# Two weight matrices of a gated MLP: w_out loaded in runs of seven rows, w_in read with a step of seven

## The chip, the cores and the metric

The kernel runs on one core of a Trainium2 chip. The metric is the device time of one execution in microseconds; the time of a kernel is the median over its runs. Before the change it is 667.86 us (three runs, 667.57 to 667.94). A core has a matrix engine (TensorE; in the profile PE for its matmuls, PEld for its weight loads), VectorE (DVE), ScalarE (ACT), GpSimd (POOL), SyncE (SP), which issues nearly all transfers here, and 16 DMA engines that carry them out. On-chip memory has 128 partitions.

## The reference

One decode step, for 4 sequences with one token each and 512 features, of a block with two halves. The first is attention of 32 heads over a cache of 4096 positions; the second, which the change touches, is a small gated MLP. All inputs are bf16.

```python
def _B_ref(x, w_in, w_sp, b_sp, w_out):
    z = _gelu(jnp.einsum('bsd,df->bsf', x, w_in))        # w_in: 512 x 1792
    z1 = z[..., :Fh].copy()                              # Fh = 896
    z2 = _layernorm(z[..., Fh:], axis=-1)
    g = jnp.einsum('ts,bsf->btf', w_sp, z2) + b_sp[None, :, None]
    return jnp.einsum('bsf,fd->bsd', z1 * g, w_out)      # w_out: 896 x 512

mod = (_silu(c) @ w_mod).reshape(c.shape[0], 6, 1, -1)   # sa, ca, ga, sb, cb, gb
h = _layernorm(x, axis=-1) * (1 + ca) + sa
x = x + ga * _A_ref(h, A_k_cache, A_v_cache, A_wq, A_wo)
h = _layernorm(x, axis=-1) * (1 + cb) + sb
x = x + gb * _B_ref(h, B_w_in, B_w_sp, B_b_sp, B_w_out)
```

The sums over the 896 hidden features (the layer norm's mean and square, and the product with w_out) do not depend on the order in which the features are stored, as long as z1, z2 and the rows of w_out share it.

## The kernel before

**The stream.** The caches are 268 MB of the 283 MB that are read. The loop `for i in range(NT)` (line 530) goes over 32 steps, each for four heads of one sequence. In a step VectorE multiplies a 4 MB tile of keys by the query (`mult`, line 288), TensorE sums it with an identity matrix as weights (`reduce_d`, line 294), VectorE and ScalarE form the softmax (`sum8`, `scores`), and two steps later TensorE multiplies by the values (`pv`, line 366). The order of the instructions on every engine is that of the program text, written out by hand (`manual_schedule`). The tiles `kt` and `vt` have two buffers each. All large transfers are issued by SP in one order, and the DMA engines take them in that order.

**The weights of the second half.** In step 30 (`if i == L - 1`, line 594) SP issues, behind the last value tile, which goes in five pieces, the transfers of `win_sb` (w_in, 1792 KB, line 597), `wout_sb` (w_out, 896 KB, line 599) and `wg_sb` (the last sixth of w_mod, 512 KB, line 602, into a buffer of `vt`, so that the profile calls it `vt`). In `win_sb` partition p holds rows 4p to 4p + 3 of w_in, each with all 1792 columns. In `wout_sb` partition p holds, in place j of NH = 7, row 128 j + p of w_out: seven rows of 1 KB that lie 128 rows apart in DRAM.

**The end.** After the loop the last pieces of values are worked off as they come (`o_last`, line 393), the attention's output is projected (line 418) and added to x, and `normed` and what follows give `hT2`, the second half's input with features on partitions (DJ = 4 groups of 128, times B = 4). Then:

- `gate(1)` and `gate(0)` (line 679) multiply by w_in: for each of seven groups f of 128 hidden features, and each k of four, one matmul (line 684) with 128 columns of `win_sb` as weights and `hT2[:, k, :]`, four columns wide, streamed. Group f holds columns `n0` to `n0 + 127`, `n0 = (h * NH + f) * P`. So hidden feature 128 f + p is on partition p, in place f.
- ScalarE takes the GELU of both halves (lines 691 and 695), after which it loads another table (line 696). Line 697 sums z2 and its square over partitions with a matmul.
- VectorE forms `zz` (line 700), the product of z1 with ones and with z2, and line 707 multiplies it by w_out: 4 groups of output features times seven places f, with `wout_sb[:, f, ...]` as weights, 128 contiguous columns each.
- Line 715 multiplies the conditioning by `wg_sb`. Lines 719 to 731 and ScalarE's lines 201 and 202 give the layer norm's scale `rs3`; lines 735 to 748 put the parts together, line 748 with the result of line 715; line 750 transposes, line 752 adds x, and SP stores the output (line 753).

Other weights are read with a step too: line 242 takes columns of `wm_sb` with a step of DJ = 4, as lines 418 and 483 do of w_o, and line 499 reads `accR`, fp32, with the same step of 4 elements.

Of the kernel before, what the change touches and what calls it, by code (L numbers as in the profile page):

```python
# [24 lines left out]
def kernel(  # L25
# [16 lines left out]
    nc = tc.nc  # L42
    P = 128
# [3 lines left out]
    FH = F // 2  # L47
    DJ = D // P
    NF = F // P
    NH = FH // P  # L50
# [22 lines left out]
    def ps_sm(shape, dtype=F32):  # L73
        return psum.tile(shape, dtype, name="sm", bufs=3)
# [37 lines left out]
    def load_v(i):  # L112
# [30 lines left out]
        out=sel32, in_=ident_f.rearrange("p (q r) -> p r q", r=R), axis=AX.X, op=ALU.add  # L143
# [10 lines left out]
    for g in range(G):  # L154
        nc.vector.tensor_reduce(out=selg[:, g:g + 1], in_=idr[:, g], axis=AX.XY, op=ALU.add)
    nc.vector.tensor_reduce(
        out=sel4, in_=ident_f.rearrange("p (c b) -> p b c", b=B), axis=AX.X, op=ALU.add
# [3 lines left out]
        out=mask8, in_=ident_f.rearrange("p (h u) -> p h u", h=2 * HQ), axis=AX.X, op=ALU.add  # L161
# [42 lines left out]
    def normed(pool, src, name, then=None, last=None):  # L204
# [24 lines left out]
        out=sg, in0=cx, scalar1=-60.0, scalar2=-1.0, op0=ALU.max, op1=ALU.mult  # L229
# [6 lines left out]
    def mod_cols(s0, n, dst):  # L236
# [20 lines left out]
        out=hs, in0=modA[:, DJ:2 * DJ, :], scalar=1.0, in1=xn, op0=ALU.add, op1=ALU.mult  # L257
# [27 lines left out]
    def mult(i, kc):  # L285
        kt = kts[i][:, kc * KC:(kc + 1) * KC, :]
        g, b = divmod(i, B)
        nc.vector.tensor_tensor(out=kt, in0=kt, in1=bc(qbc[:, g, b, :], KC), op=ALU.mult)  # L288
# [19 lines left out]
    def scores(i):  # L308
        sum8(i, 1)
        S = st.pop((i, "S"))  # L310
        mrow = wk.tile([P, 1], F32, name="mrow")
        nc.vector.tensor_reduce(out=mrow, in_=S, axis=AX.X, op=ALU.max)  # L312
        mb = wk.tile([P, R], F32, name="mb")
        nc.vector.tensor_copy(out=mb, in_=mrow.to_broadcast([P, R]))  # L314
        mt = wk.tile([P, R], F32, name="mt")
        nc.vector.transpose(mt, mb)  # L316
        nM = wk.tile([P, 1], F32, name="nM")
        nc.vector.tensor_reduce(out=nM, in_=mt, axis=AX.X, op=ALU.max)  # L318
        nc.vector.tensor_scalar(  # L319
            out=nM, in0=nM, scalar1=-att_scale, scalar2=None, op0=ALU.mult  # L320
        )
        pbd = pbds[i % 3]
        rs = wk.tile([P, 1], F32, name="rs", bufs=3)
        for q in range(HQ):
            r = slice(R * q, R * (q + 1))
            nc.scalar.activation(  # L326
                out=pbd[r, :, q], in_=S[r, :], func=AF.Exp, bias=nM[r, :],
                scale=att_scale, accum_out=rs[r, :],
            )
        st[i, "rs"] = rs  # L330
# [23 lines left out]
    def norm_b(i):  # L354
        if whole(i):
            z = st.pop((i, "z"))
            rz = wk.tile([P, z.shape[1], HQ], F32, name=f"rz{z.shape[1]}", bufs=2)
            nc.vector.reciprocal(out=rz, in_=z)
            st[i, "rz"] = rz
# [24 lines left out]
    def o_cols(i):  # L384
        op = ps_sm([P, HQ])
        nc.tensor.matmul(op, lhsT=st.pop((i, "osb")), rhs=sel4, start=True, stop=True)  # L386
        st[i, "op"] = op
# [44 lines left out]
    for n in set(SETS):  # L432
        picks[n] = consts.tile([P, n, P], BF16, name=f"pick{n}")
        for a in range(n):
            u = P // n
            nc.vector.tensor_copy(
                out=picks[n][:, :, a * u:(a + 1) * u],
                in_=ident_bf.rearrange("p (u r) -> p r u", r=n),
# [65 lines left out]
    def rows_up():  # L504
        if "rows" in st:
            wp, k = st.pop("rows")
            if k == 0:
                nc.vector.tensor_copy(out=accR, in_=wp)
            else:
                nc.vector.tensor_tensor(out=accR, in0=accR, in1=wp, op=ALU.add)  # L510
            if SETS[k + 1] == HQ:
                st["turn"] = True
# [12 lines left out]
    def add_up():  # L525
        while adds:
            o_add(*adds.pop(0))

    QPLAN = {0: (1, 2), 1: (3, 4, 5), 2: (6, 7)}
    for i in range(NT):  # L530
        more = list(QPLAN.get(i, ()))
        mult(i, 0)
        if i >= 1:
            scores(i - 1)
        if i >= 2:
            norm_b(i - 2)
        add_up()
        rows_up()
        dealt()
        if i >= 3:  # L540
            o_pick(i - 3)
        reduce_d(i, 0)
        if i >= 3:
            o_cols(i - 3)
        if more:
            queries(more.pop(0))
        mult(i, 1)
        if i >= 1:
            norm_r(i - 1)
        if i >= 3:  # L550
            o_scale(i - 3)
        sum8(i, 0)
        reduce_d(i, 1)
        load_k(i + 2)
        if i >= 1:
            norm_a(i - 1)
        project()
        if i - 3 in ends:
            deal(ends[i - 3])
        while more:  # L560
            queries(more.pop(0))
        if i >= 2:
            pv(i - 2)
        if i == 0:
            load_v(1)
        elif 2 <= i < L:
            load_v(i)
        if i == 2:
            nc.scalar.dma_start(out=sp_t[:, 0:1], in_=B_w_sp[0:1, 0:1])
            nc.scalar.dma_start(out=sp_t[:, 1:2], in_=B_b_sp.rearrange("(a b) -> a b", b=1))  # L570
            mps = ps_sm([P, 3 * DJ, B])
            mod_cols(2, 3 * DJ, mps)
            nc.vector.tensor_copy(out=modT, in_=mps)
            pre_cm.__exit__(None, None, None)
            wts = tl = ctx.enter_context(tc.tile_pool(name="wts", bufs=1))
            wo_sb = wts.tile([P, H - HQ, D], BF16, name="wo_sb")
            wo_last = wts.tile([P, HQ, D], BF16, name="wo_last")
            hl = (H - HQ) * DH
            h0 = 0
            for n in SETS:  # L580
                nc.sync.dma_start(
                    out=wo_sb[:, h0:h0 + n, :],
                    in_=A_wo[h0 * DH:(h0 + n) * DH].rearrange("(p r) n -> p r n", p=P),
                )
                h0 += n
            nc.sync.dma_start(out=wo_last, in_=A_wo[hl:H * DH].rearrange("(q p) n -> p q n", p=P))
        if i == 5:
            sps = ps_sm([P, 2])
            nc.tensor.matmul(sps, lhsT=ones_b, rhs=sp_t, start=True, stop=True)
            nc.vector.tensor_copy(out=spf, in_=sps)  # L590
            nc.vector.tensor_copy(out=g8[:, 1, :], in_=spf[:, 0:1].to_broadcast([P, B]))
            cbT = modT[:, 2 * DJ:3 * DJ, :]
            nc.vector.tensor_scalar_add(out=cbT, in0=cbT, scalar1=1.0)
        if i == L - 1:
            load_v(L)
            win_sb = wts.tile([P, DJ, F], BF16, name="win_sb")
            nc.sync.dma_start(out=win_sb, in_=B_w_in.rearrange("(p j) n -> p j n", p=P))
            wout_sb = wts.tile([P, NH, D], BF16, name="wout_sb")
            nc.sync.dma_start(out=wout_sb, in_=B_w_out.rearrange("(j p) n -> p j n", p=P))
            wg_sb = kvp.tile([P, NJ, DH], BF16, name="vt", bufs=2)  # L600
            wg_sb = wg_sb.rearrange("p n d -> p (n d)")[:, 0:DJ * D].rearrange("p (k n) -> p k n", k=DJ)
            nc.sync.dma_start(out=wg_sb, in_=wm[:, :, 5 * D:])
# [26 lines left out]
    def sums():  # L629
# [13 lines left out]
    hT2 = tl.tile([P, DJ, B], BF16, name="hT2")  # L643
# [7 lines left out]
        out=nv2, in0=mq2[:, 0:1], scalar=mq2[:, 0:1], in1=mq2[:, 1:2],  # L651
# [7 lines left out]
        out=hl, in0=xs, scalar=mq2[:, 0:1], in1=cbT[:, :, BL], op0=ALU.subtract, op1=ALU.mult  # L659
    )  # L660
    nc.vector.scalar_tensor_tensor(
        out=hT2[:, :, BL], in0=hl, scalar=rsl, in1=sbT[:, :, BL], op0=ALU.mult, op1=ALU.add
# [4 lines left out]
        out=x1m, in0=x1[:, :, :, None].to_broadcast([P, DJ, B, HQ]),  # L667
# [11 lines left out]
    def gate(h):  # L679
        z = ps_red()[:, 0:NH * B].rearrange("p (f b) -> p f b", b=B)  # L680
        for f in range(NH):
            for k in range(DJ):
                n0 = (h * NH + f) * P
                nc.tensor.matmul(
                    z[:, f, :], lhsT=win_sb[:, k, n0:n0 + P], rhs=hT2[:, k, :],
                    start=(k == 0), stop=(k == DJ - 1),
                )
        return z.rearrange("p f b -> p b f")
# [12 lines left out]
        out=zz.rearrange("p f g b -> p g b f"), in0=z1[:, None].to_broadcast([P, 2, B, NH]),  # L701
# [11 lines left out]
    for j in range(DJ):  # L713
# [7 lines left out]
        out=mq3, in_=ps3.rearrange("p (g b f) -> p g b f", g=2, b=B), axis=AX.X, op=ALU.add  # L721
# [4 lines left out]
        out=rs3, in0=mq3[:, 1], scalar=LN_EPS, in1=rs3, op0=ALU.add, op1=ALU.subtract  # L726
# [3 lines left out]
        out=g8[:, 0, :], in0=mq3[:, 0, :], scalar=-1.0, in1=g8[:, 1, :], op0=ALU.mult, op1=ALU.mult  # L730
# [5 lines left out]
        out=t3[:, 2], in0=yb[:, 0], scalar1=spf[:, 1:2], scalar2=None, op0=ALU.mult  # L736
    )
    nc.vector.tensor_tensor(
        out=g8, in0=g8, in1=rs3[:, None, :].to_broadcast([P, 2, B]), op=ALU.mult
    )  # L740
    nc.vector.tensor_tensor(
        out=t3[:, 0:2], in0=g8[:, :, :, None].to_broadcast([P, 2, B, DJ]), in1=yb, op=ALU.mult
# [3 lines left out]
        out=tt, in_=t3.rearrange("p g b j -> p b j g"), axis=AX.X, op=ALU.add  # L746
# [37 lines left out]
```

## Time and profile before

| | |
|---|---|
| median of 3 runs | 667.86 us |
| span of the profiled execution, first to last instruction | 665.8 us |
| read from memory in that span | 282.73 MB, 425 GB/s |
| busy: TensorE / its weight loads | 399.3 us (60%) / 175.4 us (26%) |
| busy: VectorE / ScalarE / GpSimd | 419.5 us (63%) / 85.0 us (13%) / 3.8 us (1%) |
| w_out: issue to landing | 26.5 us |

The times of all views are microseconds from the first instruction. A span runs from the first to the last instruction; the device time is some 2 us longer than it. The page divides the span into 40 slices and gives for each the busy tenths of every engine, the granted TensorE clock in tenths of full speed, and the share of DMA. The stretches at the end, with what each engine did (busy us, and instructions begun, in brackets):

```profile
core 0: us, PE busy (x) PEld busy (x) DVE busy (x) ACT busy (x) POOL busy (x), PEclk, DMA share, GB/s
646.70:653.20 6.50, 5.07 (x138) 4.74 (x135) 2.79 (x12) 0.00 (x0) 0.00 (x0) 0.50 1.02 425
653.20:657.70 4.50, 2.68 (x44) 2.34 (x44) 1.78 (x10) 1.74 (x5) 1.08 (x5) 0.50 0.94 354
657.70:660.00 2.30, 2.17 (x58) 2.00 (x58) 0.49 (x3) 1.16 (x4) 0.00 (x0) 0.50 0.56 199
660.00:661.40 1.40, 0.91 (x29) 0.92 (x30) 0.83 (x6) 1.36 (x3) 0.00 (x0) 0.50 0.24 78
661.40:663.20 1.80, 0.95 (x17) 0.57 (x17) 1.01 (x5) 0.02 (x1) 0.00 (x0) 0.50 0.00 0
```

The DMA engines run to about 661 us; the last 16 do not end together, so their share falls over several microseconds.

### The profile page before, as it was taken

What the parts mean: (1) busy time and instruction counts of PE and PEld (TensorE: products, weight loads), DVE (VectorE), ACT (ScalarE), POOL (GpSimd) and SP (SyncE); (2) the same over time, 40 slices, a digit from 0 to 9 for tenths busy, and PEclk for the clock granted to TensorE, in tenths of its full rate; (3) what the DMA queues carried; (4) which work ended last, traced back from release to release, by engine and by line L of the source; (5) the groups of instructions that cost most, each with busy time, mean ns of one, the idle gap of its engine ahead of it and who ended that gap; (6) DMA issues with size and microseconds to landing.
All of it is one profiled execution on the core that took longest, in us unless ns stands there. A gap on an engine that the chain in (4) does not pass through costs nothing.

```text
span 665.8 us, 6509 instructions
## 1 busy us (share of the span) xinstructions
PE 399.3 (60%) x2674; PEld 175.4 (26%) x2674; DVE 419.5 (63%) x589; ACT 85.0 (13%) x278; POOL 3.8 (1%) x17
## 2 busy tenths in 40 slices
PE   1195795556556746754665467566555468666675
PEld 0132331222222312222222222222222223322245
DVE  3485592776565777655567756657765566776833
ACT  1021120111011111101111110111111011111112
POOL 1000000000000000000000000000000000000000
PEclk9998987777898778789877778787777897887975
DMA  8999999999999999999999999999999999999996
GB/s 363 452 419 433 431 417 435 436 437 422 439 432 438 422 439 433 436 423 436 435 431 426 438 435 432 426 436 437 431 426 437 435 429 432 433 436 421 438 419 234
DMA packets 13377, 283.15 MB, mean 425 GB/s; under 512 B 1308, under 2 KB 3236, under 8 KB 4132
## 3 DMA queue, kind: packets, MB, share of 16 engines
q1 hardware_dynamic: 13328, 282.73, 98.9%
q8 instruction: 21, 0.34, 0.2%
q14 instruction: 8, 0.07, 0.0%
q10 hardware_dynamic: 20, 0.01, 0.0%
HBM read 282.73 MB, written 0.00 MB: 425 GB/s over the span
## 4 chain that ended last, share of the span: by engine, by line
DMA 56%; DVE 28%; PE 13%; issue 1%; SPq 1%; ACT 0%; DVEq 0%
DMA kt<-in_A_k_cache_dram 52%; DVE kt L288 21%; PE red L294 11%; DMA win_sb<-in_B_w_in_dram 5%; DVE osb L378 2%; DVE S L303 1%; DVE mrow L312 1%; DVE osb L374 1%; PE ops L366 1%; SPq L104 1%; DVE mt L316 1%; DVE nM L318 0%; PE qps L274 0%; DVE mb L314 0%; DVE nM L319 0%
## 5 line engine op out<-in xcount | busy, mean ns | idle before, releaser
L294 PE MATMUL red<-kt,ident_bf 128*128 128x512 bf16 x1024 | 301.5, 461 | 236.4 <-DVE kt L288 236.4
L288 DVE TENSOR_TENSOR kt<-kt,qbc 128x8192 bf16<-128x8192 bf16 x64 | 282.8, 4420 | 185.2 <-DMA kt<-in_A_k_cache_dram 184.2
L294 PEld LDWEIGHTS <-ident_bf 128*128 128x128 bf16 x1024 | 118.9, 116 | 411.5 <-issue 285.8
L326 ACT ACTIVATE pbd<-S,nM 32x128 bf16<-32x128 f32 x128 | 73.8, 577 | 505.3 <-DVE nM L319 463.2
L366 PE MATMUL ops<-vt,pbd 128*16 128x512 bf16 x992 | 62.6, 388 | 1.4 <-DMA vt<-in_A_v_cache_dram 1.4
L303 DVE TENSOR_REDUCE S<-red 128x64 f32<-128x512 f32 x64 | 43.8, 684 | 5.8 <-PE red L294 5.8
L378 DVE SCALAR_TENSOR_TENSOR osb<-ops,selg,osb 128x128 f32<-128x128 f32 x93 | 32.6, 351 | 3.3
L326 ACT ACTIVATION_READ_ACCUMULATOR pbd<-S,nM 32x1 f32 x128 | 32.0, 250 | 0.0
L366 PEld LDWEIGHTS <-pbd 128*16 128x16 bf16 x992 | 23.2, 90 | 30.7 <-issue 8.5
L386 PEld LDWEIGHTS sm<-sel,osb 128*128 128x128 f32 x62 | 11.7, 194 | 7.4 <-issue 2.2
L374 DVE TENSOR_SCALAR osb<-ops,selg 128x128 f32<-128x128 f32 x31 | 10.1, 325 | 5.3 <-PE ops L366 5.3
L386 PE MATMUL sm<-sel,osb 128*128 128x4 f32 x62 | 9.2, 219 | 2.1 <-DVE osb L378 2.0
L278 ACT CAST qbc<-qps 128x512 bf16<-128x512 f32 x8 | 4.7, 585 | 45.3 <-PE qps L274 45.3
L274 PE MATMUL qps<-wq_sb,hTb 128*32 128x512 bf16 x128 | 9.2, 412 | 1.6 <-DVE hTb L262 0.9
L312 DVE TENSOR_REDUCE mrow<-S 128x1 f32<-128x128 f32 x32 | 9.2, 286 | 1.1
L242 PE MATMUL sm<-cT,wm_sb 128*128 128x4 bf16 x80 | 3.0, 173 | 8.3 <-DMA wm_sb<-in_w_mod_dram 8.3
L316 DVE STREAM_TRANSPOSE mt<-mb 128x32 f32<-128x32 f32 x32 | 6.8, 212 | 1.1
L337 DVE TENSOR_SCALAR rsb<-mask,rs 128x4 f32<-128x4 f32 x32 | 7.2, 224 | 0.4 <-ACT pbd L326 0.4
L318 DVE TENSOR_REDUCE nM<-mt 128x1 f32<-128x32 f32 x32 | 6.0, 186 | 1.1
L314 DVE COPY mb<-mrow 128x32 f32<-128x32 f32 x32 | 5.8, 181 | 1.1
L491 PE MATMUL sm<-wo_sb,od 128*4 128x512 bf16 x24 | 5.7, 379 | 0.0
L319 DVE TENSOR_SCALAR nM<-nM 128x1 f32<-128x1 f32 x32 | 4.9, 153 | 1.1
(136 smaller groups left out, 88.8 us busy)
## 6 DMA issues: line engine op xcount, KB each, us to landing
kt<-in_A_k_cache_dram SPq DMA_DIRECT2D x31, 4096.0 KB, 23.0
vt<-in_A_v_cache_dram SPq DMA_DIRECT2D x31, 4096.0 KB, 30.7
wq_sb<-in_A_wq_dram SPq DMA_DIRECT2D x1, 4096.0 KB, 12.3
kt<-in_A_k_cache_dram SPq DMA_DIRECT2D x2, 2048.0 KB, 16.7
wo_sb<-in_A_wo_dram SPq DMA_DIRECT2D x3, 1024.0 KB, 22.9
kt<-in_A_v_cache_dram SPq DMA_DIRECT2D x3, 1024.0 KB, 25.5
wm_sb<-in_w_mod_dram SPq DMA_DIRECT2D x1, 2560.0 KB
win_sb<-in_B_w_in_dram SPq DMA_DIRECT2D x1, 1792.0 KB
```

The costliest lines, as they stand in the source:

```text
L274: nc.tensor.matmul(qp[R * q:R * (q + 1)], lhsT=hTb[:, k, b, :], rhs=wq_v[:, k, gs, q, :], start=(k == 0), stop=(k == DJ - 1), tile_positio ...
L288: nc.vector.tensor_tensor(out=kt, in0=kt, in1=bc(qbc[:, g, b, :], KC), op=ALU.mult)
L294: nc.tensor.matmul(red, lhsT=ident_bf, rhs=kt[:, :, m * RD:(m + 1) * RD], start=(m == 0), stop=(m == DH // RD - 1),)
L303: nc.vector.tensor_reduce(out=st[i, "S"][:, kc * KC:(kc + 1) * KC], in_=st.pop((i, "red", kc)), axis=AX.X, op=ALU.add,)
L312: nc.vector.tensor_reduce(out=mrow, in_=S, axis=AX.X, op=ALU.max)
L316: nc.vector.transpose(mt, mb)
L326: nc.scalar.activation(out=pbd[r, :, q], in_=S[r, :], func=AF.Exp, bias=nM[r, :], scale=att_scale, accum_out=rs[r, :],)
L337: nc.vector.tensor_scalar(out=st[g, "rsb"][:, b, :], in0=mask4, scalar1=st.pop((i, "rs")), scalar2=None, op0=ALU.mult)
L366: nc.tensor.matmul(opss[i % 2][g:g + G * HQ], lhsT=pbds[i % 3][:, n, :], rhs=vts[i][:, n, :], start=(m < 4), stop=(m >= NJ // G - 4), tile ...
L374: nc.vector.tensor_scalar(out=osb, in0=ops[:, 0, :], scalar1=selg[:, 0:1], scalar2=None, op0=ALU.mult)
L378: nc.vector.scalar_tensor_tensor(out=osb, in0=ops[:, g, :], scalar=selg[:, g:g + 1], in1=osb, op0=ALU.mult, op1=ALU.add,)
L386: nc.tensor.matmul(op, lhsT=st.pop((i, "osb")), rhs=sel4, start=True, stop=True)
```

## The change

`wout_sb` gets another arrangement: partition p holds rows 7p to 7p + 6 of w_out, which are neighbours in DRAM, in places f = 0 to 6. So that the hidden features agree, group f of `gate` no longer takes 128 neighbouring columns of w_in but every seventh one from column f of its half: hidden feature 7p + f is on partition p, in place f. The transfer of w_in, the number of instructions and the shapes of all tiles stay. Lines 691 to 707 are untouched; they work place by place.

```diff
             wout_sb = wts.tile([P, NH, D], BF16, name="wout_sb")
-            nc.sync.dma_start(out=wout_sb, in_=B_w_out.rearrange("(j p) n -> p j n", p=P))
+            nc.sync.dma_start(out=wout_sb, in_=B_w_out.rearrange("(p f) n -> p f n", p=P))
...
         for f in range(NH):
             for k in range(DJ):
-                n0 = (h * NH + f) * P
+                n0 = h * FH + f
                 nc.tensor.matmul(
-                    z[:, f, :], lhsT=win_sb[:, k, n0:n0 + P], rhs=hT2[:, k, :],
+                    z[:, f, :], lhsT=win_sb[:, k, n0:n0 + (P - 1) * NH + 1:NH], rhs=hT2[:, k, :],
                     start=(k == 0), stop=(k == DJ - 1),
                 )
```

## The prediction

> **What bounds the kernel now.** I read the page first: its span, the rows of the 40 slices, and the shares of the chain of waits.
>
> ```profile
> span 665.8 us, 6509 instructions
> PEclk9998987777898778789877778787777897887975
> DMA  8999999999999999999999999999999999999996
> DMA 56%; DVE 28%; PE 13%; issue 1%; SPq 1%; ACT 0%; DVEq 0%
> ```
>
> The DMA engines are busy in every slice but the last: the kernel streams the caches, and its end is whatever follows the last transfers. The granted clock has fallen to a half at the end. So the change must be judged in the last 9 us, and the second view is the chain of waits there, in order of time (start, length, what).
>
> ```profile
> 625.92 31.81 DMA win_sb<-in_B_w_in_dram
> 657.73 0.05 issue
> 657.78 1.67 PE red L684 x56
> 659.45 0.02 issue
> 659.47 0.19 ACT z L695
> 659.66 0.02 issue
> 659.68 1.28 ACT L696
> 660.96 0.01 issue
> 660.97 0.21 ACT rs L201
> ```
>
> The arrival of w_in lets the gate go at 657.73, its 56 matmuls of line 684 stand wholly on the chain, and then come ScalarE's GELU, a table load of 1.28 us, the reciprocal root, and some VectorE steps. w_out and the last slice of w_mod, the transfers behind w_in, are not on it. The third view is the timeline, for how close they come (in brackets idle time before, and what ended it).
>
> ```profile
> 659.69 0.40 DVE L700 TENSOR_TENSOR zz<-z,st 128x56 bf16<-128x56 f32 x1 [0.56 <-ACT z L695]
> 660.06 0.89 PEld L707 LDWEIGHTS <-wout_sb 128*128 128x128 bf16 x28 [0.29 <-DMA wout_sb<-in_B_w_out_dram]
> 660.15 0.89 PE L707 MATMUL qps<-zz,wout_sb 128*128 128x8 bf16 x28 [0.20 <-DVE zz L700]
> 661.38 0.58 PE L715 MATMUL sm<-cT,vt 128*128 128x4 bf16 x16 [0.34 <-DMA vt<-in_w_mod_dram]
> 661.87 0.21 DVE L745 TENSOR_REDUCE tt<-t 128x16 f32<-128x48 f32 x1
> 662.18 0.17 DVE L748 TENSOR_TENSOR tt<-tt,sm 128x16 f32<-128x16 f32 x1
> ```
>
> w_out is there at 660.06, and its matmuls start at 660.15, after zz (659.69 + 0.40 = 660.09): a near tie, which zz ends. The w_mod slice comes last, at 661.38; its matmuls are over at 661.96, while VectorE reaches their reader (line 748) only after line 745 ends at 662.08. So both late transfers have a little slack, 0.1 us or less, and the table load is what the end waits for.
>
> **The change, part by part.**
>
> **The load of w_out.** One DMA instruction on SP before and after, of 0.38 us at 633.5; nothing is moved past another queue. In DRAM a partition's share was seven runs of 1 KB and becomes one of 7 KB. The trace's records of single packets price this: 896 packets of 1 KB take 46 ns each, so 56 on each of 16 engines are 2.6 us; w_in's 14 KB packets take 535 ns and the 8 KB ones of the value cache 309, so a straight line between 4 KB (159 ns) and 8 KB gives about 272 ns for 7 KB, and eight of them are 2.2 us: 0.4 us less per engine. The late engines decide: the last packet of w_in ends at 657.31 and w_out's 56 follow until about 659.68, which is 2.37 us, so the last engine gains 2.37 - 2.18 = 0.2 us, for w_out and for the slice behind it. Engines that are earlier gain more, and nobody waits for them. Worth: nothing, because zz releases line 707 and the table load covers line 715. If the gate cost nothing and that cover were gone, the 0.1 us between 662.08 and 662.18 is all that the arrival could return. I take 0, with bounds -0.2 and 0. w_in lies ahead of w_out in SP's queue, and its packets are unchanged, so 657.73 stays; only early engines, which now draw larger packets while late ones still fetch w_in, could push it. The packets of 14 KB took 535 ns early and late (two of about 1.0 us apart), so I take 0, with +0.3 as the upper bound, which is how far the last engine stands behind the one before it (657.31 against 656.99).
>
> SP's issue of the w_mod slice took 6.26 us at 643.2, behind a full queue; with 768 packets fewer ahead it may be shorter. Its packets move only after 655, so this is worth 0.
>
> **The reads of w_out (line 707).** The same 28 matmuls on contiguous columns: 0. That z, z1 and zz now hold the features in another order changes no shape: lines 691 to 702 and the sums over features cost the same.
>
> **The columns of w_in (line 684).** All 56 weight loads read 128 columns at a step of seven elements (14 bytes) instead of one. No row of the trace has that step. The neighbours are steps of one and of four, and one fp32 load with columns 16 bytes apart:
>
> ```profile
> 657.78 1.65 PE L684 MATMUL red<-hT,win_sb 128*128 128x4 bf16 x56 [0.78 <-DMA win_sb<-in_B_w_in_dram]
> 76.63 1.76 PE L242 MATMUL sm<-cT,wm_sb 128*128 128x4 bf16 x48
> 649.79 0.67 PE L418 MATMUL sm<-oTs,wo_last 128*128 128x3 bf16 x16 [0.25 <-DVE oTs L408]
> 581.64 1.94 PEld L499 LDWEIGHTS sm<-ident_f,qbc 4*128 4x128 f32 x8
> 653.57 0.50 PEld L192 LDWEIGHTS sm<-sq_ln,inv_d 128*128 128x128 f32 x2
> ```
>
> The pitch of a load-and-matmul pair is the group's length less its last member's, over the members less one. Step one: (1.65 - 0.166) / 55 = 27 ns. Step four: line 242, (1.76 - 0.173) / 47 = 33.8 ns at full clock, and line 418, (0.67 - 0.172) / 15 = 33 ns at half clock. The step thus costs some 6.5 ns a pair, with the matmul as narrow as the gate's and whatever the clock. For step seven I see three readings, by the bytes of a partition that one load spans: 256 at step one, 1024 at step four, 1792 at step seven.
>
> First, a surcharge on what is spanned beyond 256 bytes: 6.5 ns for 768 more, so 13 ns for 1536 more, 40 ns a pair, 56 x 13 = +0.7 us. Second, a rate: step one has a floor of its own, and step four is already bound by its span, 33.3 ns for 1024 bytes, which makes 33.3 x 1.75 = 58 ns, 56 x 31.3 = +1.75 us. Third, the fp32 rows: line 499 has (1.94 - 0.322) / 7 = 231 ns a load, against about 0.50 - 0.31 = 0.19 us for a contiguous one; that is 41 ns for 2048 - 512 = 1536 bytes more, just the excess of our step, so 68 ns a pair and +2.3 us. That row has another type, four partitions, and only a pair to compare with, but it speaks against the smallest reading. I take the middle, 58 ns. The lower end is 27 ns (nothing; no row has a step that is quicker than none), the upper end the contiguous fp32 load at 0.19 us, 56 x 163 = +9.1 us, far off since bf16 at step four is nowhere near it.
>
> [...]
>
> All 56 pairs are on the chain: gate(1) delays line 691, gate(0) follows on TensorE and delays line 695, and behind it, on ScalarE, the table load, and then lines 201 and 202; on TensorE the sum of line 697 and then line 707, 715 and 750. Nothing beside them can take the delay up, since w_in's arrival starts the pairs and the table load waits for the last. No wait is added.
>
> **Sum.** 0 for the load, +1.75 us for the gate. The profiled execution has a span of 665.8 us, so 667.5 is due there; the median of the runs, 667.86, is 2.1 us more, which lies around the span and stays. Forecast: 667.86 + 1.75 = 669.6 us.
>
> **The rivals.** **(B) The step is cheap**, the surcharge reading or less, a pitch of 33 (as step four) to 50 ns: +0.35 to +1.3 us, 668.2 to 669.2, in the middle 668.6. For it: the two bf16 rows as they stand. Against it: the fp32 row.
>
> **(C) The step is dear**, 68 ns or more: +2.3 us, 670.2; with loads that lose their fast path altogether, toward the fp32 end (677). For it: line 499; the step is odd, so every second column starts at an odd multiple of two bytes, while all step-four columns are aligned to eight. Against the far end: line 418's loads are 118 ns long against 104, no other kind of load. [...]
>
> **(D) Not slower: the load of weights keeps its pitch at any step, and w_out's shorter transfer is what is left.** Then line 715 starts 0.1 to 0.2 us sooner, and it decides only if line 748 in truth waits for it: 667.7 to 667.9. For it: 661.38 is a DMA's release. Against it: 33 ns at step four, and 662.08 comes after 661.96. [...]
>
> That the load isn't done in 7 KB runs I hold unlikely: w_in's 14 KB runs go as one packet each.
>
> **How the numbers follow.** Forecast (50 to 63 ns) 0.42; B 0.30; C 0.18, of it 0.06 beyond 671; D 0.10. A measurement of this kernel tells 0.2%, 1.34 us, from no change; the line is at 50.6 ns. Faster by more needs an arrival that the trace doesn't show: 0.03. Within: B and the rest of D, 0.37. Slower: the forecast and C, 0.60. The range leaves out D and the far part of C: 668.0 to 671.0.
>
> **What would show it.** Line 684's 56 matmuls take 58 x 55 + 170 = 3.4 us instead of 1.65, from a start that is still at about 657.7; the table load of line 696 then starts at about 661.4. Packets of 7 KB replace w_out's, and neither line 707 nor line 715 waits for a DMA. I am wrong if line 684 stays below 2.9 us (B), goes beyond 3.8 (C), or if w_in's arrival moves.

## The result, and the profile after

The median of 12 runs is 669.34 us (668.86 to 669.97), against 667.60 us (667.28 to 668.40) in 12 runs of the kernel before: a ratio of 1.0025, 95% interval 1.0017 to 1.0034, or +1.7 us (1.1 to 2.3). The page of the kernel after has the same picture of the whole, with 768 packets fewer (12609 against 13377):

```profile
span 667.2 us, 6509 instructions
PEclk9998988777798778778977779888777897777975
DMA  8999999999999999999999999999999999999994
DMA packets 12609, 283.15 MB, mean 424 GB/s; under 512 B 1308, under 2 KB 2340, under 8 KB 3364
DMA 60%; DVE 28%; PE 10%; issue 1%; SPq 0%; ACT 0%; DVEq 0%
```

The same chain of waits at the end, in order of time (start, length, what):

```profile
625.33 32.31 DMA win_sb<-in_B_w_in_dram
657.64 0.04 issue
657.68 3.16 PE red L684 x56
660.85 0.02 issue
660.87 0.19 ACT z L695
661.06 0.02 issue
661.08 1.28 ACT L696
662.36 0.01 issue
662.38 0.21 ACT rs L201
```

The chain has the same links. w_in arrives at 657.64, 0.1 us earlier than before; line 684 takes 3.16 us where it took 1.67, and every link behind it has its old length. The timeline around it:

```profile
657.68 3.15 PE L684 MATMUL red<-hT,win_sb 128*128 128x4 bf16 x56 [0.39 <-DMA win_sb<-in_B_w_in_dram]
661.55 0.89 PE L707 MATMUL qps<-zz,wout_sb 128*128 128x8 bf16 x28 [0.20 <-DVE zz L700]
662.30 0.57 PE L715 MATMUL sm<-cT,vt 128*128 128x4 bf16 x16
663.59 0.17 DVE L748 TENSOR_TENSOR tt<-tt,sm 128x16 f32<-128x16 f32 x1
```

A pair now takes (3.15 - 0.193) / 55 = 53.8 ns; from its second pair on, the pitch is 53.3. Line 707 waits for zz alone and line 715 for nothing: both transfers behind w_in are in before they are wanted. The last VectorE step, line 752, moved from 662.83 to 664.23, 1.40 us: the 1.49 us of line 684 less the 0.1 us by which w_in came sooner in this execution.

### The profile page after: what moved, and what is told of

It reads as the page before. It is cut to its first block, busy times and chain, and to the rows that moved or that the text cites. A ratio compares the mean times of both kernels' runs of the same rounds, so it can differ in the third digit from the quotient of the medians.

```text
span 667.2 us, 6509 instructions
## 1 busy us (share of the span) xinstructions
PE 396.6 (59%) x2674; PEld 175.2 (26%) x2674; DVE 419.3 (63%) x589; ACT 85.0 (13%) x278; POOL 3.8 (1%) x17
## 2 busy tenths in 40 slices
DMA packets 12609, 283.15 MB, mean 424 GB/s; under 512 B 1308, under 2 KB 2340, under 8 KB 3364
## 4 chain that ended last, share of the span: by engine, by line
DMA 60%; DVE 28%; PE 10%; issue 1%; SPq 0%; ACT 0%; DVEq 0%
DMA kt<-in_A_k_cache_dram 55%; DVE kt L288 21%; PE red L294 9%; DMA win_sb<-in_B_w_in_dram 5%; DVE osb L378 2%; DVE S L303 1%; DVE mrow L312 1%; DVE mt L316 1%; DVE osb L374 0%; PE red L684 0%; DVE nM L318 0%; DVE mb L314 0%; DVE nM L319 0%; SPq L104 0%; ACT L696 0%
## 5 line engine op out<-in xcount | busy, mean ns | idle before, releaser
L294 PE MATMUL red<-kt,ident_bf 128*128 128x512 bf16 x1024 | 296.4, 455 | 239.7 <-DVE kt L288 239.7
L294 PEld LDWEIGHTS <-ident_bf 128*128 128x128 bf16 x1024 | 117.3, 115 | 411.6 <-issue 278.7
```

Source lines behind the costliest of these rows:

```text
L294: nc.tensor.matmul(red, lhsT=ident_bf, rhs=kt[:, :, m * RD:(m + 1) * RD], start=(m == 0), stop=(m == DH // RD - 1),)
```

## The experiments

The theory to test: the 56 weight loads are the whole loss, and the new transfer is worth nothing because it is hidden. The rivals: that the transfer has a share of its own (the median moved 1.7 us, the gate 1.5); that gate(1) has room; and three laws for what a step costs.

**One part alone: the load.** The edit against the kernel before:

```diff
-  nc.sync.dma_start(out=wout_sb, in_=B_w_out.rearrange("(j p) n -> p j n", p=P))
+  nc.sync.dma_start(out=wout_sb, in_=B_w_out.rearrange("(p f) n -> p f n", p=P))
```

> The new load of w_out without the step in the reads of w_in (so z1 and z2 meet other rows of w_out than in the reference; the work is the same). Theory, the weight loads are everything: no change, ratio within 0.05% of 1, line 684 at 1.65 us. Rival, the larger packets also move the end: faster by 0.1 to 0.2 us (0.02 to 0.03%) if line 748 waits for line 715; slower by 0.25 us (0.04%) if the early engines' larger packets delay the arrival of w_in, which would fill the gap between the 1.49 us that line 684 grew in the trace and the 1.74 us that the median moved.

667.89 us in 11 runs beside 667.55 in 27 of before: ratio 1.0002 (0.9994 to 1.0011), no difference that the interval of -0.4 to +0.7 us lets one see. Its timeline shows what becomes of the gain:

```profile
657.88 1.66 PE L684 MATMUL red<-hT,win_sb 128*128 128x4 bf16 x56 [0.43 <-DMA win_sb<-in_B_w_in_dram]
661.30 0.59 PE L715 MATMUL sm<-cT,vt 128*128 128x4 bf16 x16 [0.16 <-DMA vt<-in_w_mod_dram]
662.29 0.17 DVE L748 TENSOR_TENSOR tt<-tt,sm 128x16 f32<-128x16 f32 x1
```

Counted from the gate's start, line 715 comes after 661.30 - 657.88 = 3.42 us; before the change it was 661.38 - 657.78 = 3.60. So the last transfer does arrive 0.18 us sooner. Line 748 comes after 4.41 us here and 4.40 us before: it does not take the gain up. The interval of the time is too wide to exclude a shift of 0.3 us in the arrival of w_in; the gate started at 657.88 in this execution, at 657.78 before and at 657.68 with the whole change, in no order. The records of single packets say more. Counted from the end of the last packet of values, which are ahead of w_in in the queue, the last packet of w_in ends after 4.26 to 4.48 us in the four executions with 7 KB packets behind it, and after 4.31 to 4.57 us in three with 1 KB packets (before, the step alone, the sweep): no delay is seen.

**The other part alone: the step.** The rows of w_out go to the same places, but these lie 16 elements further apart, so each run of 1 KB stays by itself. The edit against the whole change:

```diff
-  wout_sb = wts.tile([P, NH, D], BF16, name="wout_sb")
+  wout_sb = wts.tile([P, NH, D + 16], BF16, name="wout_sb")
-  nc.sync.dma_start(out=wout_sb, in_=...)
+  nc.sync.dma_start(out=wout_sb[:, :, 0:D], in_=...)   # in_ as in the whole change
```

> The step in the reads of w_in with w_out still loaded in runs of 1 KB (the same rows in the same places, but places 16 elements apart, so that no two runs join). Theory: line 684 at 3.15 us, 53 ns a pair, and the same time as the whole change, +1.5 us over before, ratio 1.0022. Rival, the new load has a share of its own: 0.2 us away from the whole change, on either side.

669.48 us in 11 runs, ratio 1.0025 (1.0016 to 1.0034): the ratio of the whole change. Line 684 takes 3.15 us. The packets of 1 KB are back at the end (1408 of them, where the whole change has 512, those of w_mod). The interval is too wide for the rival's 0.2 us, but the timelines are not: from the gate's start to line 752 it is 5.05 us before and with the load alone, and 6.54 or 6.55 us with the step alone and with the whole change. Behind the gate's start the new load has no share.

**Half of the step.** Line 684 reads with a step of seven in gate(1) only, with the new load of w_out. The edit against the whole change:

```diff
-  n0 = h * FH + f
+  n0, s = (h * FH + f, NH) if h == 1 else (f * P, 1)   # line 684 reads n0, n0 + s, ...
```

> The new load, and the step in gate(1) alone; gate(0) reads contiguous columns (so z1 stands in the old order of features and meets z2 in the new one; the work is the same). Theory, every pair is on the chain whichever gate it is in: line 684 at 27 x 53 + 28 x 27 + 0.2 = 2.4 us, +0.75 us, ratio 1.0011. Rival, gate(1) has room, since its result is needed only for the sums of line 697, and only gate(0) counts: no change.

668.62 us in 11 runs, ratio 1.0014 (1.0005 to 1.0023), which is +0.9 us (0.3 to 1.5). Its chain:

```profile
657.60 2.42 PE red L684 x56
660.01 0.02 issue
660.03 0.19 ACT z L695
```

From the gate's start to line 695 it is 2.43 us, against 1.69 before and 3.19 with the whole change: half of the loads, half of the delay. Gate(1) has no room, because gate(0) stands behind it on TensorE and the table load behind gate(0).

**The price of a step.** Groups of 16 loads, each with a narrow matmul as in the gate, were added behind the last line of the kernel before. Each group is one line of the program and has one step.

```diff
+  sw = ps_red()[:, 0:B]
+  for r in range(16): nc.tensor.matmul(sw, lhsT=win_sb[:, r % DJ, 0:128:1], rhs=hT2[:, r % DJ, :], start=True, stop=True)
...
+  for r in range(16): nc.tensor.matmul(sw, lhsT=win_sb[:, r % DJ, 0:890:7], rhs=hT2[:, r % DJ, :], start=True, stop=True)
```

> The kernel before, with 19 groups of 16 weight loads and narrow matmuls added behind its last line, each group with another step between the columns of w_in, and three of them with 64 columns. Its whole time says nothing; the pitch inside each group does. Reading by span (33.3 ns for 1024 bytes of a partition): step 5 at 42 ns, 6 at 50, 8 at 67, 14 at 117, 56 at 467. Reading by the number of columns that share 16 bytes: 27 ns up to step 3 or so, 33 at 4, between 33 and 53 at 5 and 6, and from 8 on a flat 53, whatever the step. Reading by odd addresses: 3, 5, 7, 9 and 13 dear, 6, 8, 10, 12 and 14 no more than 33. With 64 columns half of the pitch, if the matmul's own floor allows it.

The timeline of its end, on TensorE, not all groups; lines 755 to 762 are steps 1 to 8, line 766 is 14, line 770 is 56, lines 771 and 772 have 64 columns at steps 1 and 7:

```profile
662.35 0.61 PE L755 MATMUL red<-hT,win_sb 128*128 128x4 bf16 x16
662.82 0.57 PE L756 MATMUL red<-hT,win_sb 128*128 128x4 bf16 x16
663.25 0.59 PE L757 MATMUL red<-hT,win_sb 128*128 128x4 bf16 x16
663.70 0.67 PE L758 MATMUL red<-hT,win_sb 128*128 128x4 bf16 x16
664.23 0.78 PE L759 MATMUL red<-hT,win_sb 128*128 128x4 bf16 x16
664.87 0.89 PE L760 MATMUL red<-hT,win_sb 128*128 128x4 bf16 x16
665.61 0.99 PE L761 MATMUL red<-hT,win_sb 128*128 128x4 bf16 x16
666.47 1.10 PE L762 MATMUL red<-hT,win_sb 128*128 128x4 bf16 x16
670.29 1.10 PE L766 MATMUL red<-hT,win_sb 128*128 128x4 bf16 x16
674.22 1.10 PE L770 MATMUL red<-hT,win_sb 128*128 128x4 bf16 x16
675.25 1.02 PE L771 MATMUL red<-hT,win_sb 128*64 128x4 bf16 x16
676.13 1.79 PE L772 MATMUL red<-hT,win_sb 128*64 128x4 bf16 x16
```

With 128 columns the groups grow by about a tenth of a microsecond with each step, from 0.59 at step 3 to 1.10 at step 8, and then no more. The granted clock is 0.50 through all of them, as at the gate. The starts of the single instructions, past the first few of a group, give the pitch of a pair (steps 10, 12, 13 and 16, left out here, lie between 58 and 62 ns):

| step (elements of 2 bytes) | 1 | 2 | 3 | 4 | 5 | 6 | 7 | 8 | 9 | 14 | 28 | 56 |
|---|---|---|---|---|---|---|---|---|---|---|---|---|
| ns a pair, 128 columns | 26.7 | 26.7 | 28.3 | 33.2 | 40.0 | 46.7 | 53.3 | 60.0 | 60.0 | 60.0 | 63.3 | 60.0 |

From step 4 to step 8 the pitch is 6.67 ns x (step + 1), with a floor of 26.7 ns at steps 1 and 2 (step 3, at 28.3, lies just above it) and a level of about 60 ns from 8 on. The reading by span falls (step 14 would have been 117 ns, step 56 467). That by odd addresses falls (6 and 8 are dearer than 5 and 7). What agrees in kind is the expectation by columns that share 16 bytes: with 128 columns, a step of s touches 16 s stretches of 16 bytes until each column has its own at s = 8, and that is where the growth ends (60.0 ns at steps 8, 9, 14 and 56). The runs show where it ends, not why: no run tells 16 bytes from eight elements. In size that expectation was wrong: the level is 60 ns, not 53.

**Where the transfer is not hidden.** In two kernels, both with the step, w_out is issued ahead of w_in, in runs of 1 KB (as in the step alone) and of 7 KB. The edit against the whole change, shortened:

```diff
+  wout_sb = wts.tile(...); nc.sync.dma_start(out=wout_sb..., in_=B_w_out...)
   win_sb = wts.tile([P, DJ, F], BF16, name="win_sb")
   nc.sync.dma_start(out=win_sb, in_=B_w_in.rearrange("(p j) n -> p j n", p=P))
-  wout_sb = wts.tile(...); nc.sync.dma_start(out=wout_sb..., in_=B_w_out...)
```

> The step alone, with w_out (1 KB runs) ahead of w_in in SP's queue, so that its transfer stands before the gate's start and is no longer hidden. From single packets: 56 of 1 KB on an engine are 2.4 to 2.6 us, so w_in arrives at about 660.1 to 660.3 and the time is 2.4 to 2.6 us over the whole change.

> The whole change with w_out (7 KB runs) ahead of w_in. Theory: eight packets of 272 ns are 2.2 us; w_in arrives at about 659.9, 0.2 to 0.4 us sooner than with 1 KB runs, and the time stands as much below that kernel. That is all the new load can bring where it is not hidden. Rival, 1 KB runs already go at the full rate: no difference between the two.

671.53 us (671.48 to 672.72) and 671.37 us (670.93 to 671.50), five runs each; the ratios to before are 1.0060 (1.0047 to 1.0072) and 1.0051 (1.0038 to 1.0065). They lie 2.3 and 2.1 us above the whole change (669.24 beside them), close to the 2.4 to 2.6 and 2.2 of the packets. The two medians differ by 0.16 us with intervals that overlap, and the profiled execution with 1 KB is the one that took 672.72, late already ahead of the gate. Counted from the end of the last packet of values, the last packet of w_in ends after 6.71 us with 1 KB and after 6.76 us with 7 KB, one execution each: the same within the scatter of 0.3 us seen above. So the order of the medians is the expected one, and whether 7 KB runs bring 0.2 to 0.4 us here stays open.

**Two rows instead of seven.** The sweep says that step 2 is free. So: runs of two neighbouring rows for six of the seven places, single rows for the last, and steps of two and one in the gate. The edit against the kernel before, shortened:

```diff
-  nc.sync.dma_start(out=wout_sb, in_=B_w_out.rearrange("(j p) n -> p j n", p=P))
+  nc.sync.dma_start(out=wout_sb[:, 0:6, :]..., in_=B_w_out[0:6 * P].rearrange("(g p r) n -> p g r n", p=P, r=2))
+  nc.sync.dma_start(out=wout_sb[:, 6, :], in_=B_w_out[6 * P:7 * P])
-  n0 = (h * NH + f) * P
+  n0, s = (h * FH + f // 2 * 2 * P + f % 2, 2) if f < 6 else (h * FH + f * P, 1)
```

> w_out in runs of two neighbouring rows (2 KB) for six of the seven places and single rows for the last, in two transfers, and w_in read with a step of two for those places. Theory from the sweep (26.7 ns a pair at step two): line 684 at 1.65 us and the time of before, 1.5 to 1.7 us under the whole change. Rival, that any step or the other order of rows costs something: above before by 0.3 us or more.

667.56 us in 11 runs beside 667.69 in 21 of before, ratio 0.9999 (0.9990 to 1.0008). Its gate, from the timeline (line 688 is the former 684):

```profile
657.42 1.66 PE L688 MATMUL red<-hT,win_sb 128*128 128x4 bf16 x56 [0.52 <-DMA win_sb<-in_B_w_in_dram]
```

The whole loss is gone, and nothing is won over the kernel before either: it is a tie, not a version that beats both.

**The change once more**, beside the last three:

> The whole change once more beside the other three: 1.5 to 1.8 us over before, line 684 at 3.15 us.

669.24 us in 11 runs, ratio 1.0025 (1.0017 to 1.0034), line 684 at 3.15 us.

## Why the prediction was right, step by step

**What bounds the end**: right. The gate's loads stood wholly on the chain, and half of the loads gave half of the delay.

**The load at nothing**: right. The packets of 7 KB took 272 ns each, as interpolated. The last engine was done with w_out 659.41 - 657.25 = 2.16 us after its last packet of w_in (predicted 2.18, before 2.37). The last transfer came 0.18 us sooner, within the 0.1 to 0.2 foreseen, and line 748 returned none of it. The load alone gave a ratio of 1.0002. That the larger packets push w_in back, the bound of +0.3 us, the medians can't exclude, since their intervals are some 0.6 us to either side. The gate's start scatters too: between 657.60 and 657.88 in the four executions with 7 KB packets behind w_in, and at 657.47 and 657.78 in two with 1 KB. Counted from the last packet of values, though, w_in was no later with the larger packets (4.26 to 4.48 us against 4.31 to 4.57). SP's issue of the w_mod slice did get shorter with fewer packets ahead of it, 0.56 us where it took 6.26, and 6.34 again with the step alone; as foreseen, that was worth nothing.

**The gate**: the right place and sign, a size slightly too large. The term was +1.75 us at 58 ns a pair and measured +1.49 at 53.3. What failed in it is the rate of 33.3 ns for 1024 bytes, taken from step four as if that were proportional to the span. The sweep shows, from step four to step eight, a straight line with a constant, 6.67 ns for each 256 bytes and 6.67 beside, so scaling one point overshoots. That the reading came within 5 ns is partly luck: at step 14 it gives 117 ns, where 60 was measured. The surcharge reading (40 ns) erred the other way for a reason that the sweep shows too: between steps one and four the pitch stays at its floor (26.7 ns) up to step two and has hardly left it at three (28.3), so the difference of 6.5 ns between those rows hides most of the slope.

**The rivals**: the cheap step (B, at most 50 ns) and the dear one (C, 68 or more) are both excluded by 53.3 ns in every profiled execution with the step of seven. The far end of C (677) had the fp32 rows, 0.19 us a load, as its only source, and that loads have a fast path to lose was the author's supposition: no run shows one lost, and the dearest pitch of 128 bf16 columns in the sweep is 63.3 ns. D is excluded for step seven, though for step two its premise holds: there the pitch is kept (26.7 ns) and the time is that of before (667.56 us beside 667.69). The fp32 row, whose extra time gave 68 ns, did not carry over to bf16 loads (53.3).

**The time**: 669.6 forecast, 669.34 measured. The median moved by 1.74 us and line 684 grew by 1.49; the interval of the ratio (1.1 to 2.3 us) holds both. That 1.74 is nearly the 1.75 of the forecast is luck: in the traces the way from the gate's start to line 752 grew by just 1.5 us. The rest would lie ahead of the gate, whose start differs by 0.4 us from one execution to another, and the step alone, without the new load, moved by as much (1.9 us); the runs do not show that it is anything but scatter.

## What to carry to other kernels

A layout that makes a transfer's runs longer can be paid for where the other operand is then read with a step: here 56 weight loads took twice the time (3.15 us where it was 1.65), all on the path, for a transfer that nobody waited for. The price of a step is best measured at several steps, since one neighbouring row cannot tell a floor, a slope and a level apart; in bf16 weights of 128 columns, steps up to two were free here (26.7 ns a pair), between four and eight each further one cost 6.67 ns more, and those beyond cost about as much as eight (58 to 63.3 ns beside 60.0). And a gain in a transfer counts from the instruction that waits for it last: the last transfer arrived 0.18 us sooner, but line 748, which needs it, comes at the end of the chain behind the table load (1.28 us) and started no sooner, 4.41 us after the gate's start beside 4.40.

## What the runs showed of the hardware that was not expected

Loads of 64 columns were slower than loads of 128, where half of the pitch was expected. In the sweep 64 contiguous columns took 53.3 ns a pair and 128 took 26.7; with step seven it was 104.5 against 53.3, and with step 14 116.7 against 60.0. The runs do not show why.
